# Strided attention on VectorE: a row's products in one operation and their sums in a second

## The chip, the core and the metric

The kernel runs on one core of a Trainium2 chip. Its engines work side by side, each through its own queue in order: TensorE (PE, matrix products; PEld is its loading of weights), VectorE (DVE), ScalarE (ACT), GpSimd (POOL) and SyncE (SP, which issues the DMAs). The metric is the device time of one execution in microseconds (us).

## The reference

Attention over 8 batches, 8 heads, 576 tokens of 64 channels, and then a feed-forward layer (512 to 2048 to 512) with GELU on all 4608 tokens, in float32. The first four heads attend to the last 32 tokens ("local"), the last four to every 32nd token before them ("strided"):

```python
scores = scale * np.matmul(q, k.transpose(0, 1, 3, 2))
rel = pos[:, None] - pos[None, :]
mask_local = (rel >= 0) & (rel < stride)
mask_strided = (rel >= 0) & (pos[None, :] % stride == pos[:, None] % stride)
masks = np.stack([mask_local if h < H // 2 else mask_strided for h in range(H)], axis=0)
scores = np.where(masks[None, :, :, :], scores, -1000000000.0)
attn = np.exp(scores - np.max(scores, axis=-1, keepdims=True))
attn = attn / (np.sum(attn, axis=-1, keepdims=True) + 1e-09)
x = np.matmul(attn, v)              # then (tokens, 512)
h = x @ w_in
out = (0.5 * h * (1.0 + erf(h * inv_sqrt2))) @ w_out
```

With a stride of 32 the 576 tokens of a batch are 18 rows of 32. A token in row r attends in a strided head to one token in each of the rows 0 to r, that is to r + 1 keys.

## The kernel before

**Tiles.** The tokens go in twelve tiles of 384 (12 rows of 32). For each tile the feed-forward layer runs in 16 blocks n of 128 hidden channels, 192 blocks in all. `ffn_h` (lines 619 to 621) makes H of a block with 12 matmuls, `ffn_g` applies GELU (ACT, L628), rounds it into gh (ACT, L630) and takes the rest gl = H - gh (DVE, L632), and `ffn_o` (L658 to L660) adds 9 matmuls into the three O banks of the tile. H has two PSUM banks; gh and gl have three buffers each (`gpool`). Blocks go in pairs on PE: H(n), H(n+1), O(n-2), O(n-1).

**Strided heads.** They take no part of PE, but for the first tile. A row's partitions are 4 heads x 32 tokens, and each partition needs only its own q, k and v, so DVE makes dot products along the 64 channels. The rows of all batches come in a list of visits; a unit is up to four rows (`UR`) of one visit. `strided_qk` computes a unit's scores, one fused multiply-and-add over 64 elements for each row and key (`tensor_tensor_reduce`, L494, which shows as CUSTOM_DVE_ANT_0 with an accumulator read). `sm` takes the maximum, and the exponential goes to ACT (L504). `strided_av` sums and inverts (L520 to L527), scales the weights (L524), and adds v times a weight for each row and key (L534 for the first key, L536 for the others), then transposes (L544), and `to_x` (L236, L238) rounds the result into the x of its tile as xh + xl. q, k and v of a group of visits stay in SBUF in one buffer each, as (row, channel).

**Order.** The string `START` sets, step by step, the order of the first tile: w, q, v are loads, c splits weights, f are feed-forward blocks, L, a, b, A are the first tile's attention, and u1 is the strided work of the second tile. There `alternate` mixes the three units of u1 so that steps of one row lie apart. From block 16 on, `pair` writes PE's and ACT's order by hand, while DVE's and SP's comes from the framework's scheduler. `run_strided` issues strided steps in proportion to the blocks, by a cost that each step is listed with (0.137 for a score, 0.196 for an output). The local heads (`band_job`) use PE, DVE (L311, L318 to L321) and ACT (L315). Rows on L396 to L410, L435, L438 and L441 belong to the first tile's attention, which runs on PE.

Of the kernel before, what the change touches and what calls it, by code (L numbers as in the profile page):

```python
# [10 lines left out]
F32 = mybir.dt.float32  # L11
F32R = mybir.dt.float32r
# [9 lines left out]
ALU = mybir.AluOpType  # L22
AX = mybir.AxisListType

P = 128
STRIDE = 32
TT = 384
# [6 lines left out]
UR = 4  # L34
# [29 lines left out]
ROWS = [(vi, b, r) for vi, (b, r0, r1) in enumerate(VISITS) for r in range(r0, r1)]  # L64

# [12 lines left out]
PLACE = units(UR)  # L78
# [4 lines left out]
def attn_ffn_kernel(ctx: ExitStack, tc: tile.TileContext, qk, vl, qka, va, qs, ks, vs, w, out):  # L83
# [120 lines left out]
    def small(name):  # L204
        return [lpool.tile([P, 4], F32, name=f"{k}_{name}", tag=k, bufs=4) for k in ("nm", "ss", "rs")]
# [274 lines left out]
    def strided_qk(u):  # L480
# [9 lines left out]
        for c in range(W):  # L490
            for r in range(max(0, c - r0), nr):
                def f(r=r, c=c):
                    junk = spool.tile([P, D], F32, name=f"junk_{u}_{r}_{c}", tag="junk", bufs=4)
                    nc.vector.tensor_tensor_reduce(  # L494
                        junk, sq[vi, "q"][:, r0 + r, :], sq[vi, "k"][:, c, :], 1.0, 0.0,
                        ALU.mult, ALU.add, ss[u][:, r, c:c + 1])
                ops.append((0.137, f))
# [10 lines left out]
    def strided_av(u):  # L508
# [13 lines left out]
        def quotients():  # L522
            s = ss[u][:, :, 0:W]
            nc.vector.tensor_tensor(s, s, every(z, W), ALU.mult)  # L524
            ss[u, "acc"] = spool.tile([P, UR, D], F32, name=f"acc_{u}", tag="acc", bufs=3)[:, 0:nr]
        ops += [(0.1, zsum), (0.1, lambda: nc.vector.tensor_scalar_add(z, z, 1e-9)),
                (0.1, lambda: nc.vector.reciprocal(z, z)), (0.1, quotients)]  # L527
        for c in range(W):
            for r in range(max(0, c - r0), nr):
                def f(r=r, c=c):  # L530
                    acc = ss[u, "acc"]
                    wgt = ss[u][:, r, c:c + 1]
                    if c == 0:
                        nc.vector.tensor_scalar_mul(acc[:, r, :], sq[vi, "v"][:, c, :], wgt)  # L534
                    else:
                        nc.vector.scalar_tensor_tensor(  # L536
                            acc[:, r, :], sq[vi, "v"][:, c, :], wgt, acc[:, r, :], ALU.mult, ALU.add)
                ops.append((0.196, f))
# [16 lines left out]
    def alternate(us, what, first):  # L555


        todo = []
        for u in us:
            ops = what(u)  # L560
            todo.append([[x] for x in ops[:first]] + [ops[first:-1]] + [[ops[-1]]])
        res = []
        for ops in zip(*todo):
            if len(ops[0]) == 1:
                res += [x[0] for x in ops]
                continue
            rows_ = []
            for u, x in zip(us, ops):
                r0, nr = PLACE[u][2:4]
                key = [r for c in range(r0 + nr) for r in range(max(0, c - r0), nr)]  # L570
                rows_ += [[f for k, f in zip(key, x) if k == r] for r in range(nr)]
            used = [-9] * len(rows_)
            while any(rows_):
                k = max((k for k in range(len(rows_)) if rows_[k]),
                        key=lambda k: (min(len(res) - used[k], 3), len(rows_[k])))
                used[k] = len(res)
                res.append(rows_[k].pop(0))
        return res

    def unit_job(us):  # L580

        n = 8
# [3 lines left out]
        for i in range(len(us), len(qk), n):  # L586
            for _, f in qk[i:i + n]:
                f()
            yield
# [5 lines left out]
        for i in range(0, len(av), n):  # L595
            for _, f in av[i:i + n]:
                f()
            yield
# [360 lines left out]
```

## Time and profile before

| | |
|---|---|
| time, median of 2 runs | 875.62 us (875.14 to 876.11) |
| the profiled execution, its span | 875.6 us |
| instructions | 19724 |
| DVE, busy and instructions | 707.1 us, 4901 |
| ACT, busy and instructions | 490.3 us, 1005 |
| scores L494, their accumulator reads | 1290, 1290 |
| output steps L534, L536 | 132, 1158 |

Of a group of instructions the profile gives the line, the engine, the operation, what it writes and reads, partitions x elements, the number of them, then the busy time in us and the mean of one in ns, and last the idle time of the engine just before them with what ended it. In the timeline each row begins with the start and the length in us. Successive DVE instructions overlap, so that the mean of one is longer than the distance from one start to the next. The granted clock of PE was full in nearly all of the span (0.992 on average).

### The profile page before, as it was taken

The page shows a single profiled execution, that of the slowest core. Times are in us where ns is not written, and L with a number is a line of the kernel's source. Part 1 is how long each engine was busy: PE and PEld are TensorE (multiplying, and loading weights), DVE is VectorE, ACT ScalarE, POOL GpSimd, SP SyncE. Part 2 cuts the span into 40 slices and gives each one's busy share as a digit, 9 for nine tenths or more (in the row PEclk, how much of TensorE's full clock was granted, in tenths as well). Part 3 has the DMA queues.
Part 4 walks back from the last instruction along what each step waited for, and adds up shares of the span by engine and source line. Part 5 has one row for each costly group of instructions (what it writes and reads, how often), then busy time and mean ns, then how long its engine had stood idle before and what let it go on. Part 6 is the DMA issues. An engine that isn't in the chain of part 4 may idle for free.

```text
span 875.6 us, 19724 instructions
## 1 busy us (share of the span) xinstructions
PE 853.6 (97%) x6082; PEld 768.4 (88%) x6082; DVE 707.1 (81%) x4901; ACT 490.3 (56%) x1005; POOL 17.6 (2%) x89
## 2 busy tenths in 40 slices
PE   6999999999999999999999999999999999999998
PEld 5787898899898989899889899999988988898997
DVE  6988999889989998998999879799898896751111
ACT  6978586466456274368366466546545735733222
POOL 5000100000000000000000000000000000000000
PEclk9799999999999999999999999999999999999999
DMA  9695211320310221310302221131032011000001
GB/s 350 226 372 207 96 42 24 123 76 7 128 45 19 93 75 33 98 49 8 110 28 67 67 67 43 34 123 46 8 101 79 9 34 44 32 8 6 31 1 37
DMA packets 34553, 66.68 MB, mean 76 GB/s; under 512 B 6800, under 2 KB 16528, under 8 KB 34448
## 3 DMA queue, kind: packets, MB, share of 16 engines
q1 hardware_dynamic: 34448, 65.43, 22.0%
q8 instruction: 48, 0.79, 0.4%
q14 instruction: 57, 0.47, 0.2%
HBM read 51.64 MB, written 9.44 MB: 70 GB/s over the span
## 4 chain that ended last, share of the span: by engine, by line
PE 69%; DVE 17%; DMA 5%; ACT 5%; issue 2%; SPq 2%; DVEq 0%; ACTq 0%
PE H L619 11%; PE O L659 11%; PE O L660 11%; PE H L621 11%; PE O L658 11%; PE H L620 11%; DVE acc L536 5%; DVE junk L494 4%; DMA ws<-in_w_dram 3%; DVE gl L632 2%; ACT L504 1%; SPq L326 1%; PE X_L L337 1%; ACT PT_L L315 1%; DVE xl L238 1%
## 5 line engine op out<-in xcount | busy, mean ns | idle before, releaser
L619 PE MATMUL H<-xh,w 128*128 128x384 f32 x768 | 260.8, 340 | 5.6 <-DVE gl L632 5.4
L620 PE MATMUL H<-xl,w 128*128 128x384 f32 x768 | 258.6, 337 | 0.8 <-DVE xl L238 0.8
L621 PE MATMUL H<-xh,w 128*128 128x384 f32 x768 | 258.9, 337 | 0.0
L628 ACT ACTIVATE H<-H 128x384 f32<-128x384 f32 x192 | 91.4, 476 | 287.4 <-PE H L621 230.5
L536 DVE SCALAR_TENSOR_TENSOR acc<-sv,sc,acc 128x64 f32<-128x64 f32 x1158 | 248.8, 277 | 0.6
L660 PE MATMUL O<-w,gl 128*128 128x512 f32 x576 | 226.8, 394 | 0.1
L659 PE MATMUL O<-w,gh 128*128 128x512 f32 x576 | 226.2, 393 | 0.0
L658 PE MATMUL O<-w,gh 128*128 128x512 f32 x576 | 225.0, 391 | 0.5 <-ACT gh L630 0.5
L494 DVE CUSTOM_DVE_ANT_0 junk<-sq,sk 128x64 f32<-128x64 f32 x1290 | 204.5, 217 | 3.3 <-DMA sk<-in_ks_dram 3.1
L632 DVE TENSOR_TENSOR gl<-H,gh 128x384 fp32r<-128x384 f32 x192 | 105.9, 551 | 105.8 <-ACT gh L630 105.7
L619 PEld LDWEIGHTS H<-xh,w 128*128 128x128 f32 x768 | 144.9, 189 | 12.7 <-DVE gl L632 7.5
L620 PEld LDWEIGHTS H<-xl,w 128*128 128x128 f32 x768 | 144.9, 189 | 4.8 <-DVE xl L238 1.2
L621 PEld LDWEIGHTS H<-xh,w 128*128 128x128 f32 x768 | 144.9, 189 | 0.1
L630 ACT CAST gh<-H 128x384 fp32r<-128x384 f32 x192 | 92.3, 481 | 69.2 <-PE O L659 62.8
L660 PEld LDWEIGHTS O<-w,gl 128*128 128x128 f32 x576 | 108.3, 188 | 24.4 <-DVE gl L632 1.6
L658 PEld LDWEIGHTS O<-w,gh 128*128 128x128 f32 x576 | 108.5, 188 | 21.1 <-ACT gh L630 1.0
L659 PEld LDWEIGHTS O<-w,gh 128*128 128x128 f32 x576 | 108.4, 188 | 20.6
L494 DVE DVE_READ_ACCUMULATOR2_ANT sc<- 128x1 f32 x1290 | 103.7, 80 | 0.0
L628 ACT ACT_TABLE_LOAD x62 | 79.5, 1283 | 1.1
L504 ACT ACT_TABLE_LOAD x35 | 44.9, 1283 | 0.6
L315 ACT ACTIVATE PT_L<-P_L,nm_L 128x64 f32<-128x64 f32 x132 | 44.3, 339 | 0.3
L315 ACT ACT_TABLE_LOAD x26 | 33.4, 1283 | 0.5
(114 smaller groups left out, 493.0 us busy)
## 6 DMA issues: line engine op xcount, KB each, us to landing
ws<-in_w_dram SPq DMA_DIRECT2D x16, 1023.8 KB, 9.9
qk<-in_qk_dram SPq DMA_DIRECT2D x36, 320.0 KB, 5.1
out_dram<-ob SPq DMA_DIRECT2D x34, 256.0 KB, 2.1
vl<-in_vl_dram SPq DMA_DIRECT2D x36, 192.0 KB, 3.9
sk<-in_ks_dram SPq DMA_DIRECT2D x8, 576.0 KB, 4.7
sv<-in_vs_dram SPq DMA_DIRECT2D x8, 576.0 KB, 4.0
band<-PT_L SPq DMA_DIRECT2D x240, 16.0 KB, 1.8
sq<-in_qs_dram SPq DMA_DIRECT2D x4, 576.0 KB, 4.8
```

The costliest lines, as they stand in the source:

```text
L315: nc.scalar.activation(pv[:, :, h, :], p1[:, h * 2 * QB:(h + 1) * 2 * QB].rearrange("p (c t) -> p c t", c=2), AF.Exp, bias=nm[:, h:h + 1], ...
L494: nc.vector.tensor_tensor_reduce(junk, sq[vi, "q"][:, r0 + r, :], sq[vi, "k"][:, c, :], 1.0, 0.0, ALU.mult, ALU.add, ss[u][:, r, c:c + 1])
L536: nc.vector.scalar_tensor_tensor(acc[:, r, :], sq[vi, "v"][:, c, :], wgt, acc[:, r, :], ALU.mult, ALU.add)
L619: nc.tensor.matmul(hp, w1[f][:, 0, c, :], xh[:, c, :], start=(c == 0), stop=False)
L620: nc.tensor.matmul(hp, w1[f][:, 0, c, :], xl[:, c, :], start=False, stop=False)
L621: nc.tensor.matmul(hp, w1[f][:, 1, c, :], xh[:, c, :], start=False, stop=(c == NC - 1))
L628: nc.scalar.activation(hp, hp, AF.Gelu)
L630: nc.scalar.copy(gh, hp)
L632: nc.vector.tensor_tensor(gl, hp, gh.bitcast(F32), ALU.subtract)
L658: nc.tensor.matmul(o, gh[:, sl], w2[f][:, 0, :], start=(f == 0), stop=False)
L659: nc.tensor.matmul(o, gh[:, sl], w2[f][:, 1, :], start=False, stop=False)
L660: nc.tensor.matmul(o, gl[:, sl], w2[f][:, 0, :], start=False, stop=(f == NF - 1))
```

## The change

A row's scores are computed with two operations. The first multiplies q of the row, repeated, with all its keys into a buffer of products (keys x 64), and the second adds each group of 64. Outputs go likewise: one operation multiplies v, read with the channel outside and the key inside, with the row's weights, repeated for each channel, into (64 x keys) products, and a second adds over the keys. A row is cut where it has more than 1152 products; a row of 18 keys has 1152. There is one product buffer (`NPROD`), so a product is followed by its own sums. To make place, the buffers of gl go from three to two, of the small statistics from four to three, of acc from three to two. Each product and each sum is listed with a cost of 0.15 + elements / 960. The steps of u1 go unit after unit in 5 and 6 pieces, where they went in portions of 8.

```diff
+PRODUCT = 1152
+NPROD = 1
+def cuts(n, most):
+    k = -(-n // most)
+    at = [i * n // k for i in range(k + 1)]
+    return list(zip(at, at[1:]))
+def staged(pieces, size, product, sums):
+    ops, late = [], []
+    for x in pieces:
+        c = 0.15 + size(*x) / 960
+        ops.append((1.0 * c, lambda x=x: product(*x)))
+        late.append((c, lambda x=x: sums(*x)))
+        if len(late) == NPROD:
+            ops.append(late.pop(0))
+    return ops + late
...
-        return [lpool.tile([P, 4], F32, name=f"{k}_{name}", tag=k, bufs=4) for k in ("nm", "ss", "rs")]
+        return [lpool.tile([P, 4], F32, name=f"{k}_{name}", tag=k, bufs=3) for k in ("nm", "ss", "rs")]
...
-        for c in range(W):
-            for r in range(max(0, c - r0), nr):
-                    nc.vector.tensor_tensor_reduce(
-                        junk, sq[vi, "q"][:, r0 + r, :], sq[vi, "k"][:, c, :], 1.0, 0.0,
-                        ALU.mult, ALU.add, ss[u][:, r, c:c + 1])
+        def product(r, lo, hi):
+            n = hi - lo
+            prods[r, lo] = pr = spool.tile([P, PRODUCT], F32, name=f"pq_{u}_{r}_{lo}", tag="prod", bufs=NPROD)[
+                :, 0:n * D].rearrange("p (c d) -> p c d", c=n)
+            MULT(nc).tensor_tensor(pr, sq[vi, "q"][:, r0 + r, :].unsqueeze(1).to_broadcast([P, n, D]),
+                                   sq[vi, "k"][:, lo:hi, :], ALU.mult)
+        def sums(r, lo, hi):
+            nc.vector.tensor_reduce(ss[u][:, r, lo:hi], prods.pop((r, lo)), AX.X, ALU.add)
+        ops += staged([(r, lo, hi) for r in range(nr) for lo, hi in cuts(r0 + r + 1, PRODUCT // D)],
+                      lambda r, lo, hi: (hi - lo) * D, product, sums)
...
-                        nc.vector.tensor_scalar_mul(acc[:, r, :], sq[vi, "v"][:, c, :], wgt)
-                        nc.vector.scalar_tensor_tensor(
-                            acc[:, r, :], sq[vi, "v"][:, c, :], wgt, acc[:, r, :], ALU.mult, ALU.add)
+        def product(r, lo, hi):
+            n, w_ = hi - lo, r0 + r + 1
+            prods[r, lo] = pr = spool.tile([P, PRODUCT], F32, name=f"pv_{u}_{r}_{lo}", tag="prod", bufs=NPROD)[
+                :, 0:n * w_].rearrange("p (d c) -> p d c", d=n)
+            MULT(nc).tensor_tensor(pr, sq[vi, "v"][:, 0:w_, lo:hi].rearrange("p c d -> p d c"),
+                                   ss[u][:, r, 0:w_].unsqueeze(1).to_broadcast([P, n, w_]), ALU.mult)
+        def sums(r, lo, hi):
+            nc.vector.tensor_reduce(ss[u, "acc"][:, r, lo:hi], prods.pop((r, lo)), AX.X, ALU.add)
...
-        for i in range(len(us), len(qk), n):
-            for _, f in qk[i:i + n]:
+        for part_ in pieces(qk[len(us):], 5):
+            for _, f in part_:
...
-        gl = gpool.tile([P, TT], F32R, name=f"gl_{n}", tag="gl")
+        gl = gpool.tile([P, TT], F32R, name=f"gl_{n}", tag="gl", bufs=2)
```

`MULT(nc)` is `nc.vector`. Line numbers of the changed program are larger by 22 to 36 behind the new functions.

DVE's queue in the second tile, around block 26, in the program before. junk and the sc after it are a score and its accumulator read, acc an output step, gl the subtraction of block 26; the first number in a name is the unit (or block):

```order
L632 TENSOR_TENSOR gl_26_2299<-H_26_2285,gh_26_2298 128x384
L494 ISA junk_10_1_9_2604,sc_10_2495<-sq_4_1531,sk_4_1533 128x64
L494 ISA sc_10_2495 128x1
L520 TENSOR_REDUCE z_9_95<-sc_9_2028 128x4
L494 ISA junk_10_0_10_2606,sc_10_2495<-sq_4_1531,sk_4_1533 128x64
```

And the same place now, where pv is an output product, and the reduction behind it its sums:

```order
L567 TENSOR_TENSOR pv_8_2_0_2081<-sv_4_1517,sc_8_1687 128x704
L654 TENSOR_TENSOR gl_26_2034<-H_26_2020,gh_26_2033 128x384
L571 TENSOR_REDUCE acc_8_2046<-pv_8_2_0_2081 128x64
L553 TENSOR_REDUCE z_9_95<-sc_9_1926 128x4
L567 TENSOR_TENSOR pv_8_3_0_2084<-sv_4_1517,sc_8_1687 128x768
L559 TENSOR_SCALAR z_9_95<-z_9_95 128x4
L654 TENSOR_TENSOR gl_27_2064<-H_27_2050,gh_27_2063 128x384
L571 TENSOR_REDUCE acc_8_2046<-pv_8_3_0_2084 128x64
```

Scores of unit 10 and outputs of unit 8 no longer mix; between a product and its sums there lies at most one other step or two, and gl waits behind whole products.

DVE's queue in the start, at block 11, in the program before, with output steps of the units 3, 4 and 5 in turn:

```order
L534 TENSOR_SCALAR acc_3_1343<-sv_1_1045,sc_3_967 128x64
L632 TENSOR_TENSOR gl_11_1314<-H_11_1268,gh_11_1313 128x384
L536 SCALAR_TENSOR_TENSOR acc_3_1343<-sv_1_1045,sc_3_967,acc_3_1343 128x64
L534 TENSOR_SCALAR acc_4_1345<-sv_1_1045,sc_4_969 128x64
L536 SCALAR_TENSOR_TENSOR acc_4_1345<-sv_1_1045,sc_4_969,acc_4_1345 128x64
```

And now, with unit 3 alone, row by row:

```order
L567 TENSOR_TENSOR pv_3_1_0_1319<-sv_1_1030,sc_3_967 128x128
L571 TENSOR_REDUCE acc_3_1287<-pv_3_1_0_1319 128x64
L567 TENSOR_TENSOR pv_3_2_0_1322<-sv_1_1030,sc_3_967 128x192
L571 TENSOR_REDUCE acc_3_1287<-pv_3_2_0_1322 128x64
L567 TENSOR_TENSOR pv_3_3_0_1325<-sv_1_1030,sc_3_967 128x256
L654 TENSOR_TENSOR gl_11_1289<-H_11_1244,gh_11_1288 128x384
L571 TENSOR_REDUCE acc_3_1287<-pv_3_3_0_1325 128x64
```

Product and sums of a row follow each other, and of three units in turn one is left.

More of the change, by code (lines that the diff above doesn't have):

```diff
@@ L489, in strided_qk @@
         ops.append((0.0, init))
-        for c in range(W):
-            for r in range(max(0, c - r0), nr):
-                def f(r=r, c=c):
-                    junk = spool.tile([P, D], F32, name=f"junk_{u}_{r}_{c}", tag="junk", bufs=4)
-                    nc.vector.tensor_tensor_reduce(
-                        junk, sq[vi, "q"][:, r0 + r, :], sq[vi, "k"][:, c, :], 1.0, 0.0,
-                        ALU.mult, ALU.add, ss[u][:, r, c:c + 1])
-                ops.append((0.137, f))
+        prods = {}
+        def product(r, lo, hi):
[8 more added lines that the diff above has]
+                      lambda r, lo, hi: (hi - lo) * D, product, sums)
         def sm():
@@ L524, in quotients @@
             nc.vector.tensor_tensor(s, s, every(z, W), ALU.mult)
-            ss[u, "acc"] = spool.tile([P, UR, D], F32, name=f"acc_{u}", tag="acc", bufs=3)[:, 0:nr]
+            ss[u, "acc"] = spool.tile([P, UR, D], F32, name=f"acc_{u}", tag="acc", bufs=2)[:, 0:nr]
         ops += [(0.1, zsum), (0.1, lambda: nc.vector.tensor_scalar_add(z, z, 1e-9)),
                 (0.1, lambda: nc.vector.reciprocal(z, z)), (0.1, quotients)]
[L528 to L536, printed above, removed]
-                            acc[:, r, :], sq[vi, "v"][:, c, :], wgt, acc[:, r, :], ALU.mult, ALU.add)
-                ops.append((0.196, f))
+        prods = {}
+        def product(r, lo, hi):
[6 more added lines that the diff above has]
+            nc.vector.tensor_reduce(ss[u, "acc"][:, r, lo:hi], prods.pop((r, lo)), AX.X, ALU.add)
+        ops += staged([(r, lo, hi) for r in range(nr) for lo, hi in cuts(D, PRODUCT // (r0 + r + 1))],
+                      lambda r, lo, hi: (hi - lo) * (r0 + r + 1), product, sums)
         def fin():
@@ L559, in alternate, with pieces @@
         for u in us:
[L560 to L578, printed above, removed]
+            todo.append(what(u))
+        return [ops[0] for ops in todo] + [x for ops in todo for x in ops[1:]]
     def unit_job(us):
-        n = 8
+        def pieces(ops, n):
+            for i in range(n):
+                yield ops[i * len(ops) // n:(i + 1) * len(ops) // n]
         qk = alternate(us, strided_qk, 1)
@@ L594, in unit_job @@
         av = alternate(us, strided_av, 4)
-        for i in range(0, len(av), n):
-            for _, f in av[i:i + n]:
+        for part_ in pieces(av, 6):
+            for _, f in part_:
                 f()
```

2 lines of the change are left out of this document (added).

## The prediction

> **What bounds the kernel now.** I read the page's totals first, then the stretch of each token tile, then the groups of VectorE in those stretches, and last single places of the timeline.
>
> The first rows: the engine totals, then the last shares of the chain that ended last.
>
> ```profile
> PE 853.6 (97%) x6082; PEld 768.4 (88%) x6082; DVE 707.1 (81%) x4901; ACT 490.3 (56%) x1005; POOL 17.6 (2%) x89
> PE 69%; DVE 17%; DMA 5%; ACT 5%; issue 2%; SPq 2%; DVEq 0%; ACTq 0%
> ```
>
> TensorE (PE) is busy 97% of the span, yet 17% of the chain lies on VectorE (DVE). So DVE sits just under PE: it gives little when it gets lighter and takes much when it gets heavier. The stretches show how close. Each of these ends where PE begins the next token tile (length, then busy time of PE, PEld, DVE, ACT, POOL, clock and DMA); I call them stages 1, 3, 8 and 9 of ten, and the last row is all ten.
>
> ```profile
> 98.70:173.00 74.30, 71.11 (x577) 63.92 (x577) 71.07 (x593) 46.86 (x96) 0.52 (x4) 1.00 0.22 71
> 242.50:311.80 69.30, 69.30 (x482) 62.92 (x481) 60.82 (x459) 36.39 (x79) 0.42 (x3) 1.00 0.16 50
> 589.40:662.70 73.30, 71.17 (x481) 64.26 (x480) 65.96 (x477) 39.54 (x84) 0.42 (x3) 0.98 0.16 53
> 662.70:732.60 69.90, 69.71 (x482) 62.92 (x481) 62.95 (x482) 39.31 (x81) 0.41 (x3) 1.00 0.12 38
> 98.70:801.00 702.30, 696.67 (x4802) 630.33 (x4802) 614.32 (x4590) 394.14 (x820) 4.32 (x32) 1.00 0.17 55
> ```
>
> PE needs 69.3 us a stage when nothing holds it. DVE is busy 61 to 71. Where PE lost time, it had waited for DVE: here are the two places, the subtraction gl and then the matmul that stood still (in brackets its idle time and who ended it).
>
> ```profile
> 166.07 0.55 DVE L632 TENSOR_TENSOR gl<-H,gh 128x384 fp32r<-128x384 f32 x1
> 166.67 0.45 PE L619 MATMUL H<-xh,w 128*128 128x384 f32 x1 [1.67 <-DVE gl L632]
> ...
> 654.19 0.55 DVE L632 TENSOR_TENSOR gl<-H,gh 128x384 fp32r<-128x384 f32 x1
> 654.80 0.44 PE L619 MATMUL H<-xh,w 128*128 128x384 f32 x1 [2.13 <-DVE gl L632]
> ```
>
> H has two PSUM banks, and gl reads H; a late gl keeps the bank, and the block after next cannot start. That is 1.67 + 2.13 = 3.8 us, all that a lighter DVE can give back in the stages. A gain over 2% (17.5 us, about what a measurement of this kernel can tell from no change) has no room here.
>
> **The change, part by part.** The strided heads have 132 rows with 1290 keys (1 to 18 a row). Their present cost, and the other DVE groups of the ten stages:
>
> ```profile
> L536 DVE SCALAR_TENSOR_TENSOR acc<-sv,sc,acc 128x64 f32<-128x64 f32 x1140 | 244.4, 277 | 0.6
> L494 DVE CUSTOM_DVE_ANT_0 junk<-sq,sk 128x64 f32<-128x64 f32 x1248 | 197.7, 217 | 2.5 <-DMA sk<-in_ks_dram 2.5
> L632 DVE TENSOR_TENSOR gl<-H,gh 128x384 fp32r<-128x384 f32 x161 | 88.7, 551 | 48.2 <-ACT gh L630 48.2
> L534 DVE TENSOR_SCALAR acc<-sv,sc 128x64 f32<-128x64 f32 x120 | 23.1, 247 | 2.3 <-DMA sv<-in_vs_dram 1.7
> L520 DVE TENSOR_REDUCE z<-sc 128x4 f32<-128x32 f32 (+9 forms) x34 | 6.6, 193 | 17.8 <-ACT sc L504 17.5
> ```
>
> Means of one mislead, because neighbours overlap. What counts is the distance between starts:
>
> ```profile
> 153.91 4.39 DVE L536 SCALAR_TENSOR_TENSOR acc<-sv,sc,acc 128x64 f32<-128x64 f32 x22
> ...
> 403.27 0.22 DVE L494 CUSTOM_DVE_ANT_0 junk<-sq,sk 128x64 f32<-128x64 f32 x1
> 403.42 0.08 DVE L494 DVE_READ_ACCUMULATOR2_ANT sc<- 128x1 f32 x1
> 403.42 0.22 DVE L494 CUSTOM_DVE_ANT_0 junk<-sq,sk 128x64 f32<-128x64 f32 x1
> ...
> 403.86 0.55 DVE L632 TENSOR_TENSOR gl<-H,gh 128x384 fp32r<-128x384 f32 x1
> 404.33 0.21 DVE L494 CUSTOM_DVE_ANT_0 junk<-sq,sk 128x64 f32<-128x64 f32 x1
> ...
> 410.43 0.73 DVE L534 TENSOR_SCALAR acc<-sv,sc 128x64 f32<-128x64 f32 x4
> ```
>
> A score costs 0.145 us, its accumulator read included; an output step (4.39 - 0.28) / 21 = 0.196; a first step (0.73 - 0.25) / 3 = 0.16. In all 1290 x 0.145 + 1158 x 0.196 + 132 x 0.16 = 435 us go away.
>
> What comes: per row and side one product and one reduction of 64 x keys elements. gl, 384 elements, takes 0.55 and lets the next start after 0.47: at 960 elements a us that is 0.40 plus 0.15, or plus 0.07 where the next is independent. A reduction of 192 elements, in the block of rows further down, takes 0.352: the same line. Where the next depends on it, the short chain below shows 0.17 of work and starts 0.20 apart, so 0.03 more:
>
> ```profile
> 399.47 0.17 DVE L520 TENSOR_REDUCE z<-sc 128x2 f32<-128x12 f32 x1 [0.97 <-ACT sc L504]
> 399.67 0.17 DVE L526 TENSOR_SCALAR z<-z 128x2 f32<-128x2 f32 x1
> ```
>
> There is one product buffer, so sums wait for their product and the next product for the sums. A pair therefore costs 2 x 0.0667 a key plus an overhead between 2 x 0.07 = 0.14 (another step always between) and 2 x 0.18 = 0.36 (never). The new order has a gl, a z step or a local step between about half of them: I take 0.25. Scores: 1290 x 0.133 + 132 x 0.25 = 205 us, for 187 before. There is no gain in that half: each element is now passed twice, at the price that the fused form had.
>
> Outputs: the same 205 us, for 248 before, if the product reads v at full speed. But it reads v with a step of 64 floats (256 bytes) between neighbours. The trace has no such read. The nearest rows step by 64 bytes: L441 on DVE reads one input and writes so, L438 on ACT writes so; L400 and L402 are the plain ones of the same size.
>
> ```profile
> L441 DVE TENSOR_TENSOR xl<-qka,xh 128x192 fp32r<-128x192 f32 x4 | 1.7, 492 | 0.0
> L438 ACT CAST xh<-qka 128x192 fp32r<-128x192 f32 x4 | 1.5, 522 | 0.1
> L400 DVE TENSOR_TENSOR va<-va,Am 128x192 f32<-128x192 f32 x2 | 0.7, 364 | 0.0
> L398 DVE TENSOR_REDUCE Am<-va 128x8 f32<-128x192 f32 x2 | 0.7, 352 | 0.0
> L402 ACT ACTIVATE va<-va 128x192 f32<-128x192 f32 x2 | 0.6, 358 | 0.0
> ```
>
> (492 - 364) / 192 = 0.67 ns an element on DVE, (522 - 358) / 192 = 0.85 on ACT. The ends are 0 (the write alone may be what is slow) and 0.85; I take 0.7, from the nearest row, which is a read on the same engine. That is 0.7 x 64 = 0.045 us a key, 58 us in all, and outputs cost 263.
>
> The Trainium skill bears on this twice. "SBUF — State Buffer", Specifications (TRN2), says that full bandwidth needs at least two hits in each 16-byte line and that each new line pays; by it the 256-byte step pays, as the 64-byte rows do, and the sum is the one I take. "VectorE: DVE Perf Modes", Mode 1x, has one result a cycle whatever the stride; by that the strided product would cost as the plain one.
>
> So DVE gains 205 + 263 - 435 = +33 us of work; -25 with free strides; +74 at both upper ends. It has 702.3 - 614.3 = 88 us idle in the stages, but not where it is needed. By stage: the rest of DVE's work is 614.3 less 1248 x 0.145 + 1140 x 0.196 + 120 x 0.16 = 424, 19 us a stage. To it come 0.133 a key, 0.25 a pair and 0.045 an output key, with the counts that the changed order has between the gl of each stage (score keys + output keys, pairs): stage 1: 156 + 136, 29 gives 71.3; 2: 120 + 90, 27: 57.8; 3: 129 + 131, 28: 66.6; 4: 114 + 156, 25: 68.3; 5: 150 + 105, 26: 64.2; 6: 126 + 134, 24: 65.7; 7: 116 + 119, 21: 60.9; 8: 148 + 146, 25: 71.0; 9: 151 + 150, 22: 71.4; stage 10 is light. DVE also waits for exponentials, DMAs and short steps: of the 88 us idle 48.2 are gl's and about 30 others, 3 a stage. With these, stages 1, 3, 4, 8 and 9 exceed PE's 69.3 by 5.0, 0.3, 2.0, 4.7 and 5.1: **17 us**. The 3.8 us of stalls above are the same lateness and go out of the sum. I carry no lag from a heavy stage into a light one, because of the next part.
>
> gl has two buffers instead of three. Block n's gl may now start only when the outputs of block n - 2 are done. Starts of H and O blocks on PE, and of the gl of the first:
>
> ```profile
> 303.46 0.33 PE L619 MATMUL H<-xh,w 128*128 128x384 f32 x1
> 307.64 0.39 PE L658 MATMUL O<-w,gh 128*128 128x512 f32 x1
> 309.72 0.39 PE L658 MATMUL O<-w,gh 128*128 128x512 f32 x1
> 311.76 0.33 PE L619 MATMUL H<-xh,w 128*128 128x384 f32 x1
> ...
> 306.78 0.56 DVE L632 TENSOR_TENSOR gl<-H,gh 128x384 fp32r<-128x384 f32 x1 [2.32 <-ACT gh L630]
> ```
>
> It started at 306.78 and had to be done at 311.76, when its H bank is taken again: 4.4 us of room. Now it may not start before 309.72, which leaves 1.5 us. DVE waits at that gl with its queue behind it, and a step that is late by more than 1.5 us stops PE. I price it at nothing by itself in light stages (idle DVE covers it) and at the lost carry in heavy ones.
>
> The rows of the second tile run in the hand-written start, where nothing is put between: 12 rows, 30 keys, 24 pairs x 0.36 + 60 x 0.133 + 30 x 0.045 = 18 us, for 30 x 0.145 + 18 x 0.196 + 12 x 0.16 = 10 before. DVE's idle time there:
>
> ```profile
> 50.00:98.70 48.70, 46.74 (x285) 40.25 (x284) 42.69 (x181) 38.05 (x60) 2.12 (x4) 1.00 0.65 238
> ```
>
> 6 us idle against 8 more of work: between 2 and 8 us late, I take 3 (0 if the steps fall well). The memsets, the smaller acc and statistics buffers and the cut of the hand-written work into 5 and 6 pieces I put at nothing: POOL is 2% busy, and the steps are as many as before. The SP queue has its loads of q and k a few places later; DVE's waits for them are 2.5 us in the rows above, and I leave them.
>
> Sum: the profiled span is 875.6, the median of the runs 875.62, so nothing is added around it. 875.6 + 17 - 3.8 + 3 = **892 us**.
>
> **Rivals.**
> Free strides (chance 0.27): the heaviest stages come to 65 + 3, all under 69.3, DVE's stalls go, and the start costs up to 3: 872 to 876, not slower. For it: L441's extra may be its write, as on ACT. This is the result by the skill's Mode 1x.
> Dear strides (0.25): 0.85 ns or more, with pairs that mostly wait for each other. At 0.85 and 0.36 the same stages and 5 and 6 exceed by 9.5, 4.6, 6.3, 1.8, 3.3, 8.9 and 8.9 = 43: 875.6 + 43 - 3.8 + 3 to 8 = 918 to 923. It decides from about 0.75 ns an element on, where the sum passes 893. For it: 256 bytes is further than 64.
> Parking at gl (0.10): DVE arrives early, stands until the outputs are done, and the work behind comes late. It decides where DVE has under 1 us to spare a block: with 0.3 us lost at each of 80 gl in the five heavy stages, 24 us on top of the forecast's 892, near 915. Against it: gl's idle time, 48.2 us, now costs PE nothing.
> The change might not shrink anything: the code cuts at 1152 elements, 18 keys, and the order shows products of 128x1152, so every row is one pair. I give that no chance of its own.
>
> **How the numbers follow.** The forecast has 0.38, spread over 880 to 905, a little under half of it over 893. Faster by over 2%: 0.01. Within 2%: all of free strides, 0.20 of the forecast's, 0.02 of the others: 0.50. Slower: 0.49. Range 871 to 918: it leaves out the top of dear strides and a little below free ones, some 0.15. The forecast's own range is 880 to 905.
>
> **What would show it.** The strided product: (duration - 0.15) / elements near 1.7 ns, against 1.04 for the score product; a plain 1.04 in both refutes the forecast. DVE's total near 735, not under 700. PE idle before H named to gl, in stages 1, 8 and 9 first. gl waiting for PE's O instead of ACT's gh. If PE loses time evenly in all stages, it is the parking; if DVE is lighter and PE still loses, the step that failed is the stage sum.

## The result, and the profile after

The changed kernel takes 940.37 us (939.76 to 940.98, 2 runs), the kernel before 875.62: a ratio of 1.0738, 95% interval 1.0707 to 1.0769. That is 7% slower and outside the forecast's range of 871 to 918. The profiled execution has a span of 938.0 us, 62.4 more than the 875.6 of before.

The engine totals and the last shares of the chain, from the page of the changed kernel:

```profile
PE 879.9 (94%) x6082; PEld 771.3 (82%) x6082; DVE 732.1 (78%) x1559; ACT 479.2 (51%) x997; POOL 17.6 (2%) x89
PE 50%; DVE 32%; ACT 8%; issue 6%; DMA 2%; SPq 1%; POOL 1%; DVEq 0%; ACTq 0%; POOLq 0%
```

DVE has 25 us more work (732.1 for 707.1), but the program is 62 us longer, and DVE's share of the span fell from 81% to 78%. DVE's share of the chain rose from 17% to 32%, ACT's from 5% to 8%. The engine that holds things up is not busier in proportion; it waits more. The stretches of the changed kernel (length, then busy time of PE, PEld, DVE, ACT, POOL, clock and DMA) for stages 2, 3, 8, 9, 10 and all ten:

```profile
177.40:251.10 73.70, 71.69 (x481) 63.03 (x480) 58.44 (x143) 39.14 (x83) 0.66 (x5) 1.00 0.14 46
251.10:326.30 75.20, 71.93 (x480) 63.10 (x481) 66.94 (x141) 36.69 (x80) 0.42 (x3) 1.00 0.18 61
627.10:709.20 82.10, 74.11 (x480) 65.64 (x481) 70.51 (x138) 39.19 (x83) 0.42 (x3) 0.96 0.17 55
709.20:787.20 78.00, 71.70 (x481) 62.80 (x480) 68.07 (x124) 36.57 (x79) 0.41 (x3) 1.00 0.11 34
787.20:862.20 75.00, 70.72 (x384) 62.13 (x385) 42.94 (x65) 32.52 (x69) 0.00 (x0) 1.00 0.08 24
100.90:862.20 761.30, 722.62 (x4801) 633.53 (x4800) 633.98 (x1310) 383.09 (x812) 4.28 (x32) 0.99 0.16 50
```

And stages 2 and 10 of the kernel before, which the prediction did not show:

```profile
173.00:242.50 69.50, 69.50 (x482) 62.88 (x481) 63.85 (x535) 42.27 (x86) 0.66 (x5) 1.00 0.20 67
732.60:801.00 68.40, 68.40 (x386) 61.91 (x385) 36.82 (x152) 32.59 (x69) 0.00 (x0) 1.00 0.09 27
```

The ten stages took 702.3 us and now take 761.3: 59.0 of the 62.4 us are here. The loss is in every stage, the light ones too. In stage 2 DVE has 5 us *less* work than before (58.4 for 63.9) and 15 us idle, and the stage is 4.2 us longer; in stage 10 DVE is idle for 32 of 75 us, and it is 6.6 longer. The amount of work on DVE, strides included, cannot be the reason there.

What the engines waited for, in the changed kernel (the engine and line that waited, who ended the wait, us in total, times, longest):

```profile
DVE gl L654 <- PE O L682: 91.0, 35, 5.9
PEld H L641 <- DVE gl L654: 61.0, 60, 7.0
DVE z L553 <- ACT sc L537: 44.4, 28, 4.1
PE H L641 <- DVE gl L654: 38.5, 40, 6.6
```

and in the kernel before:

```profile
DVE gl L632 <- ACT gh L630: 105.7, 45, 5.7
DVE z L520 <- ACT sc L504: 17.5, 20, 1.0
PE H L619 <- DVE gl L632: 5.4, 4, 2.1
```

gl used to wait for gh on ACT, which is early in a block; now it waits for PE's outputs, which are late in it. PE's waits for gl went from 4 to 40. DVE's waits for the exponential sc went from 17.5 us, none over 1.0, to 44.4 with one of 4.1.

One place in stage 6 shows how an idle DVE can be late. From the timeline of the changed kernel, the rows of DVE, ACT and PE apart:

```profile
491.50 0.23 DVE L553 TENSOR_REDUCE z<-sc 128x4 f32<-128x72 f32 x1 [3.05 <-ACT sc L537]
...
492.45 1.91 DVE L567 TENSOR_TENSOR pv<-sv,sc 128x960 f32<-128x960 f32 x1
...
494.39 1.15 DVE L571 TENSOR_REDUCE acc<-pv 128x64 f32<-128x960 f32 x1
...
495.55 0.53 DVE L654 TENSOR_TENSOR gl<-H,gh 128x384 fp32r<-128x384 f32 x1
```

```profile
488.90 0.47 ACT L650 ACTIVATE H<-H 128x384 f32<-128x384 f32 x1 [1.53 <-PE H L643]
489.41 0.48 ACT L652 CAST gh<-H 128x384 fp32r<-128x384 f32 x1
489.91 1.28 ACT L537 ACT_TABLE_LOAD   x1
491.20 0.26 ACT L537 ACTIVATE sc<-sc 128x72 f32<-128x72 f32 x1
```

```profile
492.70 0.40 PE L682 MATMUL O<-w,gl 128*128 128x512 f32 x1
...
494.81 0.40 PE L682 MATMUL O<-w,gl 128*128 128x512 f32 x1
496.13 0.44 PE L641 MATMUL H<-xh,w 128*128 128x384 f32 x1 [0.92 <-DVE gl L654]
```

The GELU of a block n waits for PE's H, its gh follows at 489.41, and only then comes the exponential that DVE's z step waits for, behind a load of its table that takes 1.28 us here. DVE stands there for 3.05 us. The gl of block n is in the queue behind z and behind a product and its sums of 1.9 and 1.15 us. The outputs of block n - 2 ended at 493.1 (L682's third row of them at 492.70), so gl might have started then; PE was through with the next outputs at 495.2 and wanted the H bank. In between gl had about 1.4 us to start in; it came at 495.55, and PE stood for 0.92 us.

Over 152 blocks of the second to the eleventh tile (worked out from the starts in both traces, an O taken to end 0.39 us after its last start): before, gl started ahead of the end of the outputs of block n - 2 in 109 blocks; now in none, at the median 1.35 us behind it, just where the room ends. H started on the heels of gl in 6 blocks before, in 56 now.

The strided product, in groups by form, at the largest size:

```profile
L567 DVE TENSOR_TENSOR pv<-sv,sc 128x1152 f32<-128x1152 f32 x8 | 17.9, 2239 | 0.2
L523 DVE TENSOR_TENSOR pq<-sq,sk 128x1152 f32<-128x1152 f32 x8 | 10.8, 1352 | 0.1
```

Same engine, same number of elements, plain order in and out but for v: (2239 - 1352) / 1152 = 0.77 ns an element for the step of 256 bytes. It is not paid in the shortest rows. These are the products of rows with 4 keys (256 elements) and with 3 (192):

```profile
L567 DVE TENSOR_TENSOR pv<-sv,sc 128x256 f32<-128x256 f32 x7 | 4.3, 614 | 0.2
L523 DVE TENSOR_TENSOR pq<-sq,sk 128x256 f32<-128x256 f32 x7 | 3.0, 425 | 0.2
L567 DVE TENSOR_TENSOR pv<-sv,sc 128x192 f32<-128x192 f32 x7 | 2.5, 364 | 0.2
L523 DVE TENSOR_TENSOR pq<-sq,sk 128x192 f32<-128x192 f32 x7 | 2.5, 357 | 0.2
```

With 4 keys the step costs (614 - 425) / 256 = 0.74 ns an element, with 3 almost nothing, though there too each element that is read lies at least 256 bytes from the one before. Why it sets in at 4 was not tested.

### The profile page after: what moved, and what is told of

It is laid out like the page before. It is cut to its first block, busy times and chain, and to the rows that moved or that the text cites. A ratio compares the mean times of both kernels' runs of the same rounds, so it can differ in the third digit from the quotient of the medians.

```text
span 938.0 us, 16329 instructions
## 1 busy us (share of the span) xinstructions
PE 879.9 (94%) x6082; PEld 771.3 (82%) x6082; DVE 732.1 (78%) x1559; ACT 479.2 (51%) x997; POOL 17.6 (2%) x89
## 4 chain that ended last, share of the span: by engine, by line
PE 50%; DVE 32%; ACT 8%; issue 6%; DMA 2%; SPq 1%; POOL 1%; DVEq 0%; ACTq 0%; POOLq 0%
DVE pv L567 11%; PE H L641 9%; PE H L643 8%; PE H L642 8%; PE O L681 7%; PE O L680 7%; PE O L682 7%; DVE acc L571 5%; DVE gl L654 3%; ACT L537 2%; DVE sc L527 2%; DVE pq L523 2%; DVE P_L L338 1%; ACT PT_L L342 1%; DVE xl L265 1%
## 5 line engine op out<-in xcount | busy, mean ns | idle before, releaser
L641 PE MATMUL H<-xh,w 128*128 128x384 f32 x768 | 270.0, 352 | 39.5 <-DVE gl L654 38.5
L643 PE MATMUL H<-xh,w 128*128 128x384 f32 x768 | 262.1, 341 | 1.3 <-DVE w L196 1.3
L642 PE MATMUL H<-xl,w 128*128 128x384 f32 x768 | 262.6, 342 | 0.3 <-DVE xl L265 0.3
L682 PE MATMUL O<-w,gl 128*128 128x512 f32 x576 | 228.7, 397 | 2.2 <-DVE gl L654 2.2
L680 PE MATMUL O<-w,gh 128*128 128x512 f32 x576 | 228.2, 396 | 0.0
L681 PE MATMUL O<-w,gh 128*128 128x512 f32 x576 | 228.1, 396 | 0.0
L567 DVE TENSOR_TENSOR pv<-sv,sc 128x832 f32<-128x832 f32 (+17 forms) x132 | 167.4, 1268 | 2.9
L682 PEld LDWEIGHTS O<-w,gl 128*128 128x128 f32 x576 | 108.3, 188 | 29.5 <-DVE gl L654 3.4
L527 DVE TENSOR_REDUCE sc<-pq 128x13 f32<-128x832 f32 (+17 forms) x132 | 105.6, 800 | 3.4
L571 DVE TENSOR_REDUCE acc<-pv 128x64 f32<-128x832 f32 (+17 forms) x132 | 105.7, 801 | 2.4
L523 DVE TENSOR_TENSOR pq<-sq,sk 128x832 f32<-128x832 f32 (+17 forms) x132 | 105.3, 797 | 2.2 <-DMA sk<-in_ks_dram 0.4
```

Source lines behind the costliest of these rows:

```text
L523: MULT(nc).tensor_tensor(pr, sq[vi, "q"][:, r0 + r, :].unsqueeze(1).to_broadcast([P, n, D]), sq[vi, "k"][:, lo:hi, :], ALU.mult)
L527: nc.vector.tensor_reduce(ss[u][:, r, lo:hi], prods.pop((r, lo)), AX.X, ALU.add)
L567: MULT(nc).tensor_tensor(pr, sq[vi, "v"][:, 0:w_, lo:hi].rearrange("p c d -> p d c"), ss[u][:, r, 0:w_].unsqueeze(1).to_broadcast([P, n, w ...
L571: nc.vector.tensor_reduce(ss[u, "acc"][:, r, lo:hi], prods.pop((r, lo)), AX.X, ALU.add)
L641: nc.tensor.matmul(hp, w1[f][:, 0, c, :], xh[:, c, :], start=(c == 0), stop=False)
L642: nc.tensor.matmul(hp, w1[f][:, 0, c, :], xl[:, c, :], start=False, stop=False)
```

## The experiments

Three causes were held against one another: **strides** (DVE's work), **parking** (gl with two buffers) and, later, **pace** (PE's own speed without waits); within parking, the **room** of gl and the **order** of DVE's queue. All times are medians; the ratio is to the kernel before on the same chip, with its 95% interval.

**gl with two buffers, and nothing else.** In the kernel before:

```diff
-        gl = gpool.tile([P, TT], F32R, name=f"gl_{n}", tag="gl")
+        gl = gpool.tile([P, TT], F32R, name=f"gl_{n}", tag="gl", bufs=2)
```

> The kernel before with one edit: gl has two buffers instead of three. The arithmetic and its cost stay; the scheduler places VectorE's steps anew. If the lost buffer is the main cause (the parking theory: VectorE stands at gl until the outputs of two blocks before are done, with 1.4 us of room instead of 3 to 4.4), most of the 62 us of span appear here: 900 to 925 us, with PE idle before H named to gl in all stages, and gl waiting for O of PE. If the heavier VectorE work is the main cause, the time stays near 876 to 885 us, because this kernel has no more work than before.

926.44 us, ratio 1.0594 (1.0573 to 1.0615). Its waits:

```profile
DVE gl L632 <- PE O L660: 81.0, 32, 5.8
DVE z L520 <- ACT sc L504: 58.9, 30, 4.5
DVE ss_L L318 <- ACT PT_L L315: 42.7, 23, 6.8
PE H L619 <- DVE gl L632: 37.4, 32, 3.7
```

With the old strided work, at an unchanged 707.7 us of DVE, this one number costs 51 us and brings the same three waits (and ss_L of the local heads, which waits for ACT too, goes from 10.7 us to 42.7). It is the largest cause, and it needs no change of the strided heads.

**The changed kernel with v read with step 1** (64 x keys neighbouring values of v instead of the right ones: its outputs are formed from other values of v).

```diff
-            MULT(nc).tensor_tensor(pr, sq[vi, "v"][:, 0:w_, lo:hi].rearrange("p c d -> p d c"),
+            MULT(nc).tensor_tensor(pr, sq[vi, "v"][:, 0:w_, :].rearrange("p c d -> p (c d)")[:, lo * w_:hi * w_].rearrange(
+                "p (d c) -> p d c", d=n),
```

> The changed kernel, but the output product reads v with step 1 instead of 64 floats, from the same buffer and as many elements. It so multiplies other values of v with the weights: the strided heads' outputs are left wrong in that part, only the time is read. The order on VectorE is the same, row by row. The strided products fall from 1268 ns on average to about 800 (as the score products), 62 us less VectorE work. If the stride is the main cause: back to 880 to 890 us. If the buffer of gl is: VectorE gets lighter but still parks, 905 to 925 us.

907.39 us, ratio 1.0371 (1.0352 to 1.0391). DVE is busy 673.0 us, 59 less than with the strides; a product of 1152 now takes 1356 ns, as long as a score product. So the strides cost 33 us here, and 32 remain without any. With two gl buffers, less work on DVE helps but does not save it.

**Pieces of at most 768 products, then a third gl buffer.** With 1152 a third buffer does not fit into SBUF, the memory that holds these buffers, so the pieces had to become smaller first.

```diff
-PRODUCT = 1152
+PRODUCT = 768
```

> Control for the next run: the changed kernel with a product buffer of 768 elements instead of 1152, so that rows of 13 to 18 keys go in two pieces. That frees the space that a third gl buffer needs. 48 more pairs for the scores and 48 for the outputs at about 0.25 us each make VectorE heavier by 24 us, in smaller steps. If coarse steps are what misses gl's window, it is no slower than the changed kernel or faster (925 to 940); if the amount of work is what counts, 950 to 965 us.

```diff
-        gl = gpool.tile([P, TT], F32R, name=f"gl_{n}", tag="gl", bufs=2)
+        gl = gpool.tile([P, TT], F32R, name=f"gl_{n}", tag="gl", bufs=3)
```

> The control with three buffers of gl, as the kernel before has. Parking theory: most of the loss goes although VectorE has as much work as in the control, to 895 to 915 us, and gl waits for ACT's gh again instead of O. Work theory: within 10 us of the control.

The smaller pieces alone: 934.04 us, ratio 1.0677 (1.0645 to 1.0709), 6 us less than the changed kernel although DVE has 21 us more work (753.4). With the buffer: 892.71 us, ratio 1.0205 (1.0181 to 1.0228), at the same DVE work (751.9). The buffer gives back 41 us. The waits of the second one:

```profile
DVE gl L654 <- ACT gh L652: 85.4, 30, 4.4
DVE z L553 <- ACT sc L537: 9.9, 13, 1.0
PE H L641 <- DVE gl L654: 7.1, 10, 1.4
```

gl waits for gh again, the waits at z fall from the 25.3 us of the kernel with smaller pieces alone to 9.9, and PE's from its 29.0 to 7.1.

**More room by PE's order instead of by a buffer.** Outputs of a block between the two H of a pair: H(n), O(n-2), H(n+1), O(n-1). Now only one block of outputs lies between the H of a block and the gl that may follow.

```diff
         others(n)
-        ffn_h(n + 1)
-        g = ffn_g(n + 1)
-        next(g)
         if n >= NB + 2:
             ffn_o(n - 2)
-        for _ in g:
+        ffn_h(n + 1)
+        for _ in ffn_g(n + 1):
             pass
```

In the changed kernel, gl still with two buffers:

> The changed kernel with another order of blocks on PE and nothing else: H(n), O(n-2), H(n+1), O(n-1) instead of H(n), H(n+1), O(n-2), O(n-1). gl still has two buffers, and its waits are the same ones, but the buffer of gl(n) comes free one block earlier against the moment when H's bank is taken again: 4.15 us of room less 0.6 for gl itself, 3.5 us, where it has 1.4. Parking theory: most of the loss goes without a third buffer and without less work: 890 to 905 us. If the two buffers cost only because the scheduler then places VectorE's steps badly, or if the work is the cause, it stays at 925 to 940.

In the kernel before:

> The kernel before with the alternating order of blocks on PE (three buffers of gl). It had 3.8 us of PE stalls at gl and some at the start: with more room for gl they should go, 870 to 874 us. Nothing to gain beyond that, since PE is busy 97%. If alternation costs PE something itself, over 876.

In the kernel before with two gl buffers:

> The kernel before with two buffers of gl (926 us in the first experiment) and the alternating order of blocks. Parking theory: the arithmetic being the old one, nothing is left of the loss, 872 to 880 us. If two buffers cost by the scheduler's other placement, 900 or more.

899.70 us (ratio 1.0270, 1.0249 to 1.0290); 876.29 (1.0004, 0.9992 to 1.0016); 886.36 (1.0119, 1.0092 to 1.0145). So this order of PE's blocks gives nothing where gl has three buffers, and 40 us in both kernels where it has two. It adds no buffer and takes no work away; it widens the time in which gl may start, from some 1.4 us to 3.5. That is the parking, seen from a second side. In the last of the three, gl starts as late behind the outputs of block n - 2 as without the new order (at the median 1.4 us and 1.3), but H starts on its heels in 4 of the 152 blocks instead of 46.

The middle one missed its expectation of a small gain. Its trace has PE's waits for gl down from 5.4 us to 1.7, but each undisturbed stage takes 69.8 us for 69.3: from one start to the next, an O matmul takes 2.2 ns more than in the kernel before and an H matmul 1.0 (worked out as under Pace below). So this order costs PE about what it gives back. The last stayed some 10 us above before instead of meeting it; it has the same slower pace and 7.7 us of waits for gl.

**Room or order.** With gl's new wait, the scheduler orders DVE's queue differently. Around block 26 in the kernel before, on DVE, the z step of a strided unit stands behind the block's gl:

```order
L632 TENSOR_TENSOR gl_26_2299<-H_26_2285,gh_26_2298 128x384
...
L520 TENSOR_REDUCE z_9_95<-sc_9_2028 128x4
...
L632 TENSOR_TENSOR gl_27_2336<-H_27_2322,gh_27_2335 128x384
```

With two buffers and nothing else changed, it stands ahead of it:

```order
L520 TENSOR_REDUCE z_9_95<-sc_9_2028 128x4
...
L632 TENSOR_TENSOR gl_26_2299<-H_26_2285,gh_26_2298 128x384
```

So it is, by one gl, for all 33 units from unit 7 on, and for the same 33 between the two kernels with pieces of 768. A z step waits for ACT's exponential, that stands behind a GELU, that waits for H on PE, that waits for the bank that a gl frees. With a gl behind z in DVE's queue, a late gl can make the next z late, and that z the gl behind it. In the kernel with two buffers, each z step was therefore tied to the gl that it follows in the kernel before:

```diff
-            nc.vector.tensor_reduce(z, ss[u][:, :, 0:W], AX.X, ALU.add)
+            ins = nc.vector.tensor_reduce(z, ss[u][:, :, 0:W], AX.X, ALU.add)
+            if u >= 7:
+                tc.add_manual_dep(ins.ins, gl_of[AFTER[u - 7]].ins.name, mybir.DependencyInfo(
+                    mybir.DependencyClass.Sync, mybir.DependencyReason.DATA), reason="order")
```

> The kernel before with two gl buffers, as in the first experiment (926.4 us), but each strided unit's z step, which waits for the exponential on ACT, is made to stand behind the gl that it stands behind in the kernel before. With two buffers the scheduler had put it one gl earlier for every unit from the second tile's on. Order theory (DVE stands at z with a gl behind it, and that makes PE late): DVE's waits at z return to under 25 us, most of the 50 us goes, 878 to 895. Room theory (gl has some 1.4 us between the end of PE's outputs and the moment at which PE wants the H bank, and any late step uses it up): gl still waits for O, and 915 to 928 remain.

899.47 us, ratio 1.0271 (1.0251 to 1.0291): neither theory's range. DVE's waits, and PE's:

```profile
DVE gl L638 <- PE O L666: 102.6, 40, 5.8
DVE ss_L L318 <- ACT PT_L L315: 44.3, 29, 5.3
DVE z L523 <- ACT sc L507: 5.4, 7, 1.0
```

```profile
PE H L625 <- DVE gl L638: 18.3, 21, 2.4
```

The waits at z are gone, and with them 27 of the 51 us; gl still waits for O, and 24 us stay. Against this stands the last run with the alternating order, the kernel before with two gl buffers. By the starts in its trace, each z step but one stands where it stands with two buffers alone, one gl early, and z still waits long:

```profile
DVE z L520 <- ACT sc L504: 51.7, 28, 4.1
PE H L619 <- DVE gl L632: 7.7, 5, 3.5
```

Yet 40 of the 51 us are gone there. So the early z costs much only where the room is narrow, and the two shares, 27 and 40 of 51, do not add up: order and room act on each other, and no part of the loss belongs to one alone. Nor are the 24 us left here the room by itself. The ss_L steps of the local heads also stand one gl earlier with two buffers, 30 of 33 by the starts in the traces, in this run too, and still wait 44.3 us. To tie these back was not tried.

**Third buffer and step 1 together.** Both edits in one (outputs from other values of v):

> Product buffer of 768, three buffers of gl and v read with step 1 (other values of v, so the strided heads' outputs are wrong; only the time is read). Both causes away. If parking and the amount of VectorE work together are all of it: 874 to 880 us, the time before. If coarse steps or the exponentials' waits cost something by themselves: 885 or more.

882.91 us, ratio 1.0084 (1.0062 to 1.0106). DVE has less work than before (695.7 us) and PE's H no longer waits for gl, but 7 us stayed. The remainder is in stages where no engine is waited for: the stretch 453.9 to 524.3 of this kernel is PE without a gap, 70.4 us where it was 69.3. So PE itself was slower.

**Pace.** In the last tile DVE has almost nothing to do and PE does the same 355 matmuls in every kernel. The stretch of the last tile in the kernel before, in the changed one and in the last experiment, each from its own windows:

```profile
801.00:875.60 74.60, 70.67 (x355) 63.68 (x353) 8.92 (x16) 18.82 (x38) 0.00 (x0) 0.99 0.07 22
```

```profile
862.20:938.00 75.80, 71.99 (x355) 64.21 (x353) 9.48 (x17) 18.82 (x38) 0.00 (x0) 1.00 0.07 22
```

```profile
804.90:880.60 75.70, 71.95 (x355) 64.23 (x353) 8.92 (x16) 18.80 (x38) 0.00 (x0) 1.00 0.06 21
```

The same work at the same granted clock takes 1.2 us longer. Worked out from all starts between 180 and 860 us (distances under 0.26 us), an H matmul starts 174.5 ns after the one before in the kernel before and 176.7 in the changed one, an O matmul 228.9 and 233.9. For a block of 12 and 9 that is 0.071 us, for a stage of 16 blocks 1.1, the 69.3 to 70.4 above. What PE reads in the last tile lies where it lay, except the weights: they stand behind the small statistics buffers, of which the change took three away, and begin 32 bytes off the multiple of 64 at which they began. To test this, unused bytes were put ahead of the weights; with them the weights move, and the local heads' small buffers, which the last tile does not use. Every engine's order stays as it was.

```diff
     lpool = ctx.enter_context(tc.tile_pool(name="lpool", bufs=2))
+    lpool.tile([P, 8], F32, name="pad", tag="pad", bufs=1)
```

> The kernel before with 32 unused bytes a partition ahead of the weight buffers, every engine's order unchanged. In the last tile of the changed kernel and of its variants, where DVE has next to nothing to do, PE starts an H matmul every 176 ns and an O matmul every 234, against 173 and 227 in the kernel before and in the variant of it with two gl buffers. Their weight buffers begin 32 bytes off a multiple of 64 bytes, since the smaller statistics buffers stand ahead of them; those of the two others begin on one. Placement theory: this kernel's matmuls go to 176 and 234, stages from 69.3 to about 70.5, the time to 886 to 892. Rival (the pace comes from something else in the changed program, its DVE work or its instructions): 173 and 227 remain, 875 to 877.

> The changed kernel with the same 32 bytes, so that its weights begin on a multiple of 64 bytes again; orders unchanged. Placement theory: matmuls back at 173 and 227; the stages are set by the loop through gl more than by PE, so some 6 to 14 of the 65 us come back, 926 to 934. Rival: 939 to 942.

> The changed kernel with products of at most 768 elements, three gl buffers and the 32 bytes (892.7 without them). Placement theory: 878 to 884; what remains over the kernel before is the price of the strided read. Rival: 892 to 893.

> As the last one, but v read with step 1 (its outputs are therefore formed from other values of v): 882.9 without the 32 bytes. Placement theory: the 7 us that were left over against the kernel before are the slower matmuls, and go: 869 to 875. Rival: 882 to 884.

882.68 us (ratio 1.0072, 1.0057 to 1.0087); 939.37 (1.0730, 1.0710 to 1.0750); 891.46 (1.0174, 1.0156 to 1.0191); 875.87 (0.9997, 0.9982 to 1.0012). The first and the last say that the place of the buffers matters: 32 bytes that nobody uses cost the kernel before 7 us and give the other 7 us back. But the theory as put was too simple, in its numbers too. In the kernel before only O got slower (174.2 and 232.5 ns); in the others H got faster and O hardly (173.6 and 232.9 in the last). The changed kernel gained 1 us instead of 6 to 14, and the next one 1 instead of 9 to 15: where PE waits for gl, a faster PE waits longer (38.5 to 40.0 us in the changed kernel, 7.1 to 11.2 in the next).

So other distances were tried: 64 and 128 bytes in the kernel before, and 96 bytes in the two others, which brings the weights back to their old place modulo 512.

> The kernel before with 64 unused bytes a partition ahead of the weight buffers, which then begin at 448 modulo 512 (384 in the kernel before, 416 with 32 bytes). If each start other than the one of the kernel before costs pace: H 173, O 231 to 234, 880 to 884. If only a multiple of 64 matters: H 173, O 227, 875 to 877.

> The kernel before with 128 unused bytes, weights at a multiple of 512. If the place matters modulo 128 (or less): 173 and 227, 875 to 877. If modulo 256 or 512: O slower, 880 to 884.

> The changed kernel with products of at most 768 elements, three gl buffers and 96 unused bytes, so that the weights begin at 384 modulo 512 as in the kernel before (892.7 us with none, 891.5 with 32 bytes). If the place sets the pace: 173 and 227, and 885 to 889; what then remains over the kernel before is the strided read and the second buffer-free order of DVE. If it does not: 890 to 893.

> As the last one, but v read with step 1 (outputs from other values of v; 882.9 with no unused bytes, 875.9 with 32). If the place sets the pace: 173 and 227, 868 to 873, below the kernel before. If not: 875 to 877.

877.85 us (ratio 1.0040, 1.0020 to 1.0060); 884.23 (1.0098, 1.0080 to 1.0117); 888.29 (1.0146, 1.0124 to 1.0169); 871.34 (0.9947, 0.9927 to 0.9967). The paces: 174.2 and 229.2 ns with 64 bytes, 176.1 and 232.5 with 128, and 174.3 and 229.0 in the last, as in the kernel before. The last tile of the kernel before with 32 bytes and with 128, and of the last one:

```profile
806.10:881.20 75.10, 71.31 (x355) 63.62 (x353) 8.92 (x16) 18.78 (x38) 0.00 (x0) 1.00 0.07 22
```

```profile
807.00:882.40 75.40, 71.57 (x355) 64.09 (x353) 8.92 (x16) 18.80 (x38) 0.00 (x0) 1.00 0.06 22
```

```profile
795.10:869.60 74.50, 70.65 (x355) 63.65 (x353) 8.91 (x16) 18.79 (x38) 0.00 (x0) 1.00 0.07 22
```

That the place sets the pace is shown, in both directions. By which rule is not: modulo 512, the O matmuls were fast at 384 and 448 and slow at 0, 288, 320 and 416, the H matmuls slow at 0 and 288 only. The kernel with 64 bytes did not behave by either expectation: the pace was nearly that of before, and the time still 0.4% longer.

The last two kernels of that set also differ in the strides alone, with all else as before. Their totals, the strided one first:

```profile
PE 854.0 (96%) x6082; PEld 765.2 (86%) x6082; DVE 751.0 (85%) x1751; ACT 494.2 (56%) x1009; POOL 17.5 (2%) x89
```

```profile
PE 848.7 (98%) x6082; PEld 766.4 (88%) x6082; DVE 695.1 (80%) x1751; ACT 494.2 (57%) x1009; POOL 17.4 (2%) x89
```

56 us of strides on DVE cost 17 us of time.

**The whole computation with all three causes taken out.** v is laid out in memory with the key innermost, one contiguous block for each visit, so that the product reads it with step 1 (this is done ahead of the kernel and is not in its time); three gl buffers, pieces of 768, 96 unused bytes.

```diff
+                flat = t[:, o:o + r1, :].rearrange("p c d -> p (c d)")
+                sq[vi, nm] = flat.rearrange("p (d c) -> p d c", c=r1)
+                at = sum(x[2] for x in VISITS[:vi]) * D
+                nc.sync.dma_start(flat, src[:, at:at + r1 * D])
...
-            MULT(nc).tensor_tensor(pr, sq[vi, "v"][:, 0:w_, lo:hi].rearrange("p c d -> p d c"),
+            MULT(nc).tensor_tensor(pr, sq[vi, "v"][:, lo:hi, 0:w_],
...
+        "vs": np.concatenate([by_row(v)[b, :, :r1].transpose(0, 2, 1).reshape(P, -1) for b, _, r1 in VISITS], axis=1),
```

> The whole computation, with all three causes taken out: three gl buffers (products of at most 768 elements), weights at 384 modulo 512, and v laid out with the key innermost before it is loaded, one contiguous block for each visit, so that the product reads it with step 1. If the step of v is what is left (888.3 with step 64 floats, 871.3 with step 1 from other values of v): 869 to 873, a little below the kernel before. If it is not, or the loads of v in blocks cost: 876 or more.

871.71 us, ratio 0.9960 (0.9940 to 0.9980): as expected, and a little below the kernel before. In its twin above, with step 1 from other values of v, PE is busy 98% of the span, so there is hardly more to win this way.

The 65 us from end to end, along one path (the order of the steps matters, since lateness and room act on each other): 875.3 to 871.3 for two passes with step 1 (-4), to 888.3 with the strides (+17), to 892.7 with the weights moved (+4), to 934.0 with two gl buffers (+41), to 940.4 with pieces of 1152 (+6). Along another path, from before: two gl buffers alone +51.

## Why the prediction was wrong

**The step that failed** is "gl has two buffers instead of three ... I price it at nothing by itself in light stages (idle DVE covers it) and at the lost carry in heavy ones". The prediction had the right rows, the 4.4 us of room and the 1.5 that would be left, and drew the wrong sum from them. It measured 51 us alone and 41 on top of the rest. Two things were overlooked. Idle time of a queue in order is not a reserve: DVE cannot do its next steps while it stands at gl or z, and 11.3 of the 15 us that it is idle in stage 2 are waits at these two. And the new wait changed the order of DVE's queue: with two buffers z and ss_L came to stand one gl earlier than with three, in the kernel before and in the one with pieces of 768. The z waits rose from 17.5 to 58.9 us with the old strided work, and they are 44.4 in the changed kernel. Taking back the order of z alone gave 27 of the 51 us, more room alone 40: the loss is made by the two together, and how it divides between them stays open.

The rival **parking at gl** named this mechanism, with a chance of 0.10 and a size of 24 us from 0.3 us at 80 blocks of five heavy stages. The narrow room was right, the new order was not in it; the size was less than half, and it was put into five heavy stages, where it decides in light ones too. "Against it: gl's idle time, 48.2 us, now costs PE nothing" was the wrong witness: that idle time was waiting for gh, early in the block.

**The strides** were priced well. 0.77 ns an element for the 0.7 taken, and 59 us of DVE's work for the 58. By the distances between starts, scores went from 188 us to 202 and outputs from 252 to 264, where the working has 187 to 205 and 248 to 263: so there is no gain in the score half, as it said. DVE gained 25 us for the 33; the sign "near 735" is not the working's own 707.1 + 33 = 740, and 732.1 is under both. The Trainium skill's "SBUF — State Buffer", Specifications (TRN2), asks for two hits in each 16-byte line; the strided read pays here, with 0.74 to 0.83 ns in rows of 4 keys and more. In rows of 2 and 3 keys, where each element lies in another line than the one before it too, it costs next to nothing, and there the trace does not agree. The Trainium skill's "VectorE: DVE Perf Modes", Mode 1x, read in the prediction so that the step does not matter, did not hold for the longer rows. **Free strides** falls with that. **Dear strides** had the step at 0.85 ns or more and pairs that mostly wait for each other; the step is above the 0.75 from which it was to decide, but the work came out below the forecast's, and its 918 to 923 was passed only by another cause: the changed kernel without the step still takes 907.

**The stage sum**, 17 us for strides and pairs less 3.8, comes near in size once the other causes are out: 888.3 us, in pieces of 768 and so with 19 us more DVE work, is 13 above the kernel before, where the forecast's 892 was 16 above. That is luck in part, since it does not hold in place. It laid the loss into stages 1, 8 and 9. In that kernel stages 1 and 8 are shorter than before (71.7 us for 74.3 and 71.6 for 73.3), and the loss is spread over others, with 70 to 73 us in each of the first nine stages (tile starts at 101.9, 173.6, 244.2 and so on to 743.4).

**The start**, priced at 3 us, took 2.2 (the first H of the second tile at 100.9 for 98.7).

**"The memsets, the smaller acc and statistics buffers ... I put at nothing"** was wrong by a route that no row of before hints at: the statistics buffers moved the weights, and PE's pace with them. It is 12 us where PE is the bound (882.9 to 871.3), and 4 beside the strides.

By its own list of signs, four came true: the strided product, DVE's total, gl waiting for O, PE idle before H named to gl (in all ten stages, most in the eighth). "If PE loses time evenly in all stages, it is the parking" is the sign that decided: from tile start to tile start every stage is longer, by 2.2 us (the first) to 8.8 (the eighth).

## What to carry to other kernels

When a change takes a buffer away, write down for each step that uses it when it may start at the earliest and when it must start at the latest, and compare what is left with the longest piece of work and the longest wait on its engine; idle time of that engine counts for nothing while its queue stands at that step, and a scheduler that sees the new wait may move other waits ahead of it, which costs most where the room is narrow. A change in layout has side effects of its own: give the buffers back one at a time, and look at a stretch where nothing waits to see whether an engine's bare pace is still the same.

## What the hardware showed that was not expected

PE's pace depends on where its weight buffers lie in SBUF: 128 unused bytes ahead of them, with the same instructions in the same order, make 9 us of 875, and 96 bytes in another kernel take 12 away. The granted clock does not show it, nor does any wait. The distances between starts go from 174.5 to 176 ns for H, and from 229 to 232 or 234 for O. Which rule of addresses stands behind it stays open.

On DVE, a read with a step of 256 bytes costs 0.74 to 0.83 ns an element more than a plain one of the same size in rows of 4 keys and more, and next to nothing in rows of 2 and 3 (291 ns for 293 with 2 keys, 364 for 357 with 3). The 64-byte steps of the kernel before, in one input and in the output, cost about as much (0.67). And more work was less time once: pieces of 768 instead of 1152 added 21 us to DVE and took 6 off the program. The waits at z fell from 44.4 to 25.3 us with it; that gl stands behind shorter pieces would explain this, and was not tested apart.
